# Half sums and differences of keys kept in two query buffers, and output halves added on VectorE

## The chip, the cores and the metric

The kernel runs on one core of one Trainium2 chip, in one launch. The core has five engines with instruction streams of their own: TensorE (PE, with its weight loads PEld), VectorE (DVE), ScalarE (ACT), GpSimd (POOL) and SyncE (SP), which only issues DMAs here. Each engine works through its stream in the order in which the program was written, and waits where a semaphore holds an instruction back. The metric is device time in microseconds, the median of several executions; the profile is one further execution.

## The reference

Two attention branches over the same 2048 x 512 input are mixed by a gate:

```
qkv = x @ wqkv                       # branch A: 32 heads of 16
logits = q . k[pos - 2*w], w = 0..7  # 8 keys behind each position, dilated by 2
a = softmax(logits) @ v @ wo_a
q = x @ wq; k = x @ wk; v = x @ wv   # branch B: 32 query heads, one key/value head
b = softmax(q k^T / 4) @ v @ wo_b    # all 2048 keys for all 2048 queries
out = g * a + (1 - g) * b            # g = sigmoid(x . gate_w)
```

Branch B is the bulk: 32 x 2048 x 2048 scores, their exponentials, and their sums weighted with v. All is float32.

## The kernel before

**Units and steps.** Branch B is cut into 32 units (NU): four blocks of 512 queries (NQB) times eight groups of four heads (NHG). A unit has 16 steps, one for each 128 keys, so phase 2 has 512 steps (NS). In each step `exp_pair` (line 443) makes scores for two pairs of heads, in the banks eb[0] and eb[1] (e0, e1), and ScalarE takes their exponentials into SBUF (tile pexp, six buffers); `weighted` (line 455) multiplies those of the step before with v and adds them up in the bank po. After a unit's 16 steps `finish_a` (line 470) transposes po on VectorE, and GpSimd scales it with the gate.

**Maxima.** Softmax subtracts the maximum over the keys, which must be known before a unit's first step. So all scores are computed twice: a *fill* is a matmul of 128 queries by 512 keys of one head (62 of the 64 rows of one half of the array; the two halves work side by side for the two heads of a couple) and a maximum over its 512 columns. There are 2048 fills (NF), 64 per unit. `fill_pair` (line 326) makes two in the double bank m2 with one reduce on VectorE (line 331); `fill_one` (line 335) makes one in the bank m1 (line 342). Results land in a small tile mx per unit, made by `unit_tile` (line 301). When a unit is full, `filled` (line 316) reduces it once more (lines 321, 323) and `shift_a` to `shift_d` write minus the maximum into two spare rows of the unit's query buffer, so that the scores come out shifted.

**Pairs.** During phase 1 (projections), fills may take another form: with half sums and half differences of two blocks of keys (tile kcd, made by `half_keys` and `half_parts`, lines 363 and 375), the maximum of two scores is the half sum plus the absolute half difference. `fill_diff` (line 392) makes two difference matmuls in m2 and two Abs on ScalarE into dd; `fill_sum` (line 404) makes one sum matmul in m1 or po and one fused add-and-maximum on VectorE. A pair covers four fills, and of each two columns of mx it writes only one. `paired` says when this form is possible: an even position, its half sums formed, nothing left over in `half`. Phase 1 ends by emptying `formed`.

**Query buffers.** Units sit in eight buffers qst (NB). `stack(u)` (line 277) loads unit u by four DMAs on SP's queue as soon as the unit eight before it has ended.

**The order of the work** is written out by a planner that runs while the program is built: it keeps a clock for PE, ACT and DVE (`clk`, `after`, with the durations in line 45) and emits a fill where a bank is free by that clock. In the loop from line 992 every step emits e0's scores, a fill in m2, e1's scores, a fill in m1 if the rest needs it (line 1023: `ahead` counts two fills for every step to come, and eleven for each output row to come), then the weighted sums. Each engine keeps exactly that order.

**Output blocks.** The 16 output rows of 128 tokens come in four blocks of four, between steps (`out_phase`, line 707). A block starts when the units that it needs are shaped, branch A's half is done, and the lead of the fills falls under LEAD units or a latest step is reached; `prepare` stands one step ahead of it. `stream` (line 670) runs the two halves of the array side by side over the row's items (24 for each half, 21 in the last block) and puts fills between them. `turn` transposes branch A's rows; `out_store` (line 650) copies both halves of the output bank to SBUF on ScalarE (line 654), adds them on GpSimd (line 658) and stores the row. The last block runs while the last units are still at work, and keeps its rows in SBUF (line 668) until the end.

**Branch A** runs on GpSimd throughout (`work`, line 832), which also loads the output weights (`extra`).

Of the kernel before, what the change touches and what calls it, by code (L numbers as in the profile page):

```python
# [6 lines left out]
F32 = mybir.dt.float32  # L7
# [6 lines left out]
P = 128  # L14
# [22 lines left out]
NB = 8  # L37
# [3 lines left out]
NH = NJ // 2  # L41
LEAD, M2S, M1S = 1.5, 0.5, 0.3

# [5 lines left out]
def gated_mix_kernel(ctx, tc, xt, wa, wk, wq, wo_a, wo_b, out):  # L49
# [15 lines left out]
    mk = cp.tile([P, 8], F32, name="mk")  # L65
    qst = [cp.tile([P, 2, 512], F32R, name=f"qst{k}") for k in range(NB)]

# [209 lines left out]
    def stack(u):  # L277
        qb, hg = divmod(u, NHG)
        for b in range(2):
            hi, lo = (qd[s, :, qb, 4 * hg + 2 * b:4 * hg + 2 * b + 2, :].rearrange("d c n -> d (c n)") for s in range(2))  # L280
            ap = [list(x) for x in hi.ap]
            twice = bass.AP(tensor=hi.tensor, offset=hi.offset, ap=[ap[0], [0, 2]] + ap[1:])
            dst = qst[u % NB].rearrange("p c n -> p (c n)").bitcast(F32)
# [17 lines left out]
    def unit_tile(v):  # L301
        if v not in mx:
            mx[v] = wp.tile([P, 2, 2, 4, 4], F32, name="mx", bufs=3)
            if v <= NB:
                nc.scalar.activation(mx[v].rearrange("p b i t k -> p (b i t k)"), ident[:, 0:64], AF.Identity, scale=0.0, bias=mk[:, 6:7])
            left[v] = NF // NU
        return mx[v]

    def max_mm(dst, v, pr, t, kc, odd):
        b = 64 * odd  # L310
        nc.tensor.matmul(dst, qst[v % NB][b:b + 62, pr, t * P:(t + 1) * P], kst[b:b + 62, kc * 512:(kc + 1) * 512], start=True, stop=True)  # L311

# [62 lines left out]
    def half_parts(g, keys):  # L375
        for x in range(2):
            nc.scalar.activation(kcd[0][:, g, x], hb[g][x], AF.Identity, scale=mk[:, 0:1])
            at = after("act", clk["pe"], 0.65)
        for x in range(2):
            parts = kcd[0][:, g, x]  # L380
            nc.vector.scalar_tensor_tensor(parts, hb[g][x], mk[:, 1:2], parts.bitcast(F32), op0=ALU.mult, op1=ALU.add)
            free[keys[x]] = after("dve", at + 0.1, 0.7) + 0.1
        formed.add(g)

    def paired():
        return len(slots) > 1 and slots[0][3] % 2 == 0 and slots[0][3] // 2 in formed and slots[1] == slots[0][:3] + (slots[0][3] + 1,) and fillable()

    def half_mm(dst, v, pr, t, kc, x, odd):
        b = 64 * odd
        nc.tensor.matmul(dst, qst[v % NB][b:b + 62, pr, t * P:(t + 1) * P], kcd[0][b:b + 62, kc // 2, x, :], start=True, stop=True)  # L390

    def fill_diff():
        v, pr, t, kc = slots.pop(0)
        slots.pop(0)
        for odd in range(2):
            half_mm(m2[:, odd, :], v, pr, t, kc, 1, odd)
        at = after("pe", 0, T_R) + T_LAT
        for odd in range(2):
            nc.scalar.activation(dd[0][:, odd], m2[:, odd, :], AF.Abs)  # L399
# [33 lines left out]
    def shift_d(v, ml, k):  # L433
        b, g = divmod(k, 4)
        dst = qst[v % NB][64 * b + 62:64 * b + 64].rearrange("x i (t q) -> x i t q", t=4).bitcast(F32)
# [7 lines left out]
    def exp_pair(s, pr):  # L443
        bank, key = eb[pr], f"e{pr}"
        u, kt = divmod(s, NJ)
        for odd in range(2):
            b = 64 * odd
            nc.tensor.matmul(bank[:, odd, :], kst[b:b + 64, kt * P:(kt + 1) * P], qst[u % NB][b:b + 64, pr, :], start=True, stop=True)  # L448
        e = px.tile([P, 2, 512], F32, name="pexp", bufs=6)
        nc.scalar.activation(e, bank, AF.Exp, scale=SCALE)  # L450
# [199 lines left out]
    def out_store(j, n, k):  # L650
        nonlocal pool
        del turned[j, 0], turned[j, 1]
        two = p2b[0].tile([P, 2, D], F32, name="two", bufs=2)
        nc.scalar.activation(two, eb[k], AF.Copy)
        free[f"e{k}"] = after("act", clk["pe"] + T_LAT, 0.92)
        pool = max(pool, 1e3 * clk["act"]) + 1300
        if n == C:
            nc.gpsimd.tensor_add(two[:, 0], two[:, 0], two[:, 1])
            nc.sync.dma_start(out[0].rearrange("(p j) d -> p j d", j=NJ)[:, j, :], two[:, 0])
        else:  # L660
            x = len(parts)
            if x < 2:
                spare.append(p2[0].tile([P, 512], F32, name="part", tag=("own", "tr8")[x], bufs=1))
            elif x == 2:
                own = p2[0].tile([P, 2, 512], F32, name="part", tag="pr", bufs=1)
                spare.extend([own[:, 0, :], own[:, 1, :]])
            parts[j] = spare[x]
            nc.gpsimd.tensor_add(parts[j], two[:, 0], two[:, 1])

# [36 lines left out]

    def out_phase(js, n):

# [13 lines left out]
        def done(at):  # L722
            x, j, i = at
            if i % 4 == 3:
                run_tasks()
                run_pool()
            if x == 0 and i == 1:
                turn(j, 1)
# [103 lines left out]
    def work():  # L832
# [38 lines left out]
        for i in range(0, len(order), 2):  # L871
# [17 lines left out]
            yield from load(i + 3)  # L889
            if p2b and extra:  # L890
                for f, a in extra.pop(0):
                    f(*a)
                yield 1300
        assert not extra
# [199 lines left out]
```

## Time and profile before

| | |
|---|---|
| median of 3 runs | 1521.74 us (1521.68 to 1521.97) |
| profiled execution | 1523.47 us |
| its span, first to last instruction | 1521.7 us |
| granted TensorE clock | 0.998 |
| phase 1 | to 282 us |
| output blocks | from 865, 1131, 1270 and 1426 us |
| last step | to 1508 us |

In the profile, `L331` is line 331 of the kernel, `mx<-pm` means that a tile mx is written from the bank pm, and `x562` counts instructions. The banks are named by their tiles: pe is e0 and e1, pm is m2, ps is m1. A row of a group has busy time and mean duration, then the idle time of the engine ahead of it with what ended it. In the timeline a row has start, duration, engine, line, operation; "[0.83 <-ACT mx L305]" says that the engine was idle for 0.83 us until that ACT instruction ended. A row of a window has its bounds and length, then busy time and number of instructions of each engine (or of one line's alone), the granted clock, the share of DMA time and GB/s.

### The profile page before, as it was taken

The numbers are of one execution on the slowest core, as the hardware profiler recorded it, in microseconds if no ns is written. First come the engines' busy times: TensorE is split into PE (matmuls) and PEld (weight loads), VectorE is DVE, ScalarE is ACT, GpSimd is POOL, SyncE is SP. The second block draws the span as 40 slices with busy tenths as digits, with TensorE's granted clock in tenths as the row PEclk, the third lists the DMA queues.
The fourth block names the chain that finished last, engine by engine and source line by source line (L and its number), as shares of the span: only waits on it lengthen the run. The fifth ranks groups of instructions, "written<-read, shape, count | busy, mean of one in ns | idle before, by whom it ended". The sixth has DMA issues, their size and how long they took to land.

```text
span 1521.7 us, 29098 instructions
## 1 busy us (share of the span) xinstructions
PE 1490.4 (98%) x11020; PEld 708.1 (47%) x11020; DVE 1236.0 (81%) x1748; ACT 1245.8 (82%) x1590; POOL 1035.8 (68%) x1773
## 2 busy tenths in 40 slices
PE   7999999999999999999999999999999999999998
PEld 4889888533333333333333453333345335433532
DVE  6976666789889888889888998898989889887811
ACT  4558987889999999999999759999974995799676
POOL 7866987787888888988888888889888003100210
PEclk9999999999999999999999999999999999999999
DMA  6744223121121120220211112102101000000000
GB/s 216 203 116 134 87 73 121 44 75 47 40 86 43 44 76 19 69 63 25 75 54 35 61 40 68 46 34 69 50 30 34 6 2 15 16 2 1 1 2 28
DMA packets 43908, 85.63 MB, mean 56 GB/s; under 512 B 9520, under 2 KB 25960, under 8 KB 39672
## 3 DMA queue, kind: packets, MB, share of 16 engines
q1 hardware_dynamic: 36200, 44.00, 9.7%
q0 software_dynamic: 6560, 37.95, 7.4%
q8 instruction: 86, 1.41, 0.4%
q10 hardware_dynamic: 1008, 1.84, 0.3%
q14 instruction: 54, 0.44, 0.1%
HBM read 57.97 MB, written 25.25 MB: 55 GB/s over the span
## 4 chain that ended last, share of the span: by engine, by line
PE 88%; ACT 6%; DVE 4%; issue 1%; DMA 1%; POOL 0%; SPq 0%; DVEq 0%; ACTq 0%; POOLq 0%
PE po L458 31%; PE pe L448 22%; PE pm L311 9%; PE pe L943 9%; PE ps L311 8%; PE pe L719 5%; ACT pexp L450 3%; ACT dd L399 2%; DVE mx L331 2%; PE pm L390 1%; PE pe L174 1%; PE po L390 1%; PE ps L390 1%; DVE mx L342 1%; DMA xraw<-xt 1%
## 5 line engine op out<-in xcount | busy, mean ns | idle before, releaser
L450 ACT ACTIVATE pexp<-pe 128x1024 f32<-128x1024 f32 x1024 | 991.8, 1022 | 93.1 <-PE pe L448 91.7
L331 DVE TENSOR_REDUCE mx<-pm 128x2 f32<-128x1024 f32 x562 | 686.3, 1221 | 134.3 <-PE pm L311 129.8
L458 PE MATMUL po<-pexp,vst 128*32 128x512 f32 x4096 | 545.5, 605 | 1.2 <-ACT pexp L450 0.6
L448 PE MATMUL pe<-qst,kst 64*128 64x512 f32 x2048 | 465.6, 450 | 7.1 <-ACT pexp L450 3.9
L448 PEld LDWEIGHTS pe<-qst,kst 64*128 64x128 f32 x2048 | 191.3, 183 | 513.5 <-ACT pexp L450 503.3
L342 DVE TENSOR_REDUCE mx<-ps 128x1 f32<-128x512 f32 x553 | 376.1, 680 | 4.9 <-PE ps L311 4.1
L311 PE MATMUL pm<-kst,qst 62*128 62x512 f32 x1137 | 237.8, 408 | 3.0 <-DVE mx L331 2.4
L311 PE MATMUL ps<-kst,qst 62*128 62x512 f32 x553 | 224.4, 406 | 0.8 <-DVE mx L342 0.8
L518 POOL TENSOR_TENSOR pr<-aext 128x256 f32<-128x256 f32 x256 | 182.0, 737 | 0.2
L578 POOL TENSOR_TENSOR oa<-oa,av 128x256 f32<-128x256 f32 x224 | 163.9, 732 | 15.4
L458 PEld LDWEIGHTS po<-pexp,vst 128*32 128x32 f32 x4096 | 80.6, 108 | 178.2 <-issue 164.9
L575 POOL TENSOR_TENSOR av<-aext,lg 128x256 f32<-128x256 f32 x224 | 139.2, 622 | 12.8
L484 POOL TENSOR_TENSOR rl<-rl,gate_t 128x16 f32<-128x16 f32 x31 | 6.8, 220 | 197.9 <-DVE rl L478 197.8
L311 PEld LDWEIGHTS pm<-kst,qst 62*128 62x128 f32 x1137 | 109.6, 186 | 26.8 <-DVE mx L331 22.6
L311 PEld LDWEIGHTS ps<-kst,qst 62*128 62x128 f32 x553 | 102.9, 186 | 25.4 <-DVE mx L342 20.3
L399 ACT ACTIVATE dd<-pm 128x512 f32<-128x512 f32 x166 | 92.2, 610 | 22.5 <-PE pm L390 11.4
L943 PE MATMUL pe<-wah,xh 64*128 64x384 f32 (+1 forms) x504 | 109.2, 343 | 0.0
L943 PE MATMUL pe<-wal,xh 64*128 64x384 f32 (+1 forms) x504 | 108.9, 341 | 0.0
L943 PE MATMUL pe<-wah,xl 64*128 64x384 f32 (+1 forms) x504 | 108.9, 341 | 0.0
L409 DVE CUSTOM_DVE_ANT_0 dd<-ps,dd 128x512 f32<-128x512 f32 x83 | 57.4, 692 | 60.5 <-PE ps L390 30.3
L250 POOL TENSOR_TENSOR stage<-stage,two 128x384 f32<-128x384 f32 x64 | 64.9, 1014 | 29.9 <-ACT two L241 15.5
L524 POOL TENSOR_TENSOR tr<-pr 128x512 f32<-128x512 f32 x64 | 81.7, 1276 | 4.2
(168 smaller groups left out, 1594.2 us busy)
## 6 DMA issues: line engine op xcount, KB each, us to landing
aext<-ad POOLq DMA_DIRECT2D x32, 1056.0 KB, 5.4
ad<-stage SPq DMA_DIRECT2D x32, 384.0 KB
qst<-qd SPq DMA_DIRECT2D x64, 128.0 KB
xraw<-xt SPq DMA_DIRECT2D x16, 256.0 KB
qd<-qhi SPq DMA_DIRECT2D x16, 256.0 KB
qd<-qlo SPq DMA_DIRECT2D x16, 256.0 KB
qst<-qd SPq DMA_DIRECT2D x64, 64.0 KB
qst<-ml SPq DMA_DIRECT2D x228, 2.0 KB
```

The lines of the kernel that those rows point to most:

```text
L311: nc.tensor.matmul(dst, qst[v % NB][b:b + 62, pr, t * P:(t + 1) * P], kst[b:b + 62, kc * 512:(kc + 1) * 512], start=True, stop=True)
L331: nc.vector.tensor_reduce(m[:, :, pr, t, kc], dst, AX.X, ALU.max)
L342: nc.vector.tensor_reduce(m[:, odd, pr, t, kc:kc + 1], dst, AX.X, ALU.max)
L399: nc.scalar.activation(dd[0][:, odd], m2[:, odd, :], AF.Abs)
L448: nc.tensor.matmul(bank[:, odd, :], kst[b:b + 64, kt * P:(kt + 1) * P], qst[u % NB][b:b + 64, pr, :], start=True, stop=True)
L450: nc.scalar.activation(e, bank, AF.Exp, scale=SCALE)
L458: nc.tensor.matmul(po[32 * i:32 * i + 32, :], vst[:, kt, :], pexp[s, i // 2][:, i % 2, :], start=(kt == 0), stop=(kt == NJ - 1))
L518: nc.gpsimd.tensor_mul(pr[:, k], q, e[:, o:o + NH, AC:2 * AC])
L524: nc.gpsimd.tensor_add(nx, cur[:, :, 0:n], cur[:, :, n:2 * n])
L575: nc.gpsimd.tensor_mul(av, e[:, o:o + NH, 2 * AC:].rearrange("p j (h d) -> p j h d", d=DH), lg[:, w].unsqueeze(3).to_broadcast([P, NH, AG, ...
L578: nc.gpsimd.tensor_add(ao, ao, av)
L943: nc.tensor.matmul(front[2 if x == last else x % 2][0][:, b, :n], l[h], r[h], start=(i == 0), stop=(i == 3 * C - 1))
```

## The change

Two stores keep the half sums and differences in DRAM while phase 1 makes them. At step 132 one load brings them back, over the two query buffers 6 and 7; from unit 14 on the units share the six others (`home`). Three output blocks, those of whole rows, start at the second step of a unit and take their fills as pairs, with the bank po (empty at that point) and with two dd tiles in turn. No single fill is made at the first step of a unit. Since pairs now occur among all units, every unit's mx gets its start value from ScalarE. `out_store` copies only one half of the bank, and VectorE adds the other to it. Blocks start at a lead of 3.0 instead of 1.5 units; the planner counts 20 fills for each whole row instead of eleven; GpSimd takes up to two loads of output weights at a time instead of one.

```diff
-LEAD, M2S, M1S = 1.5, 0.5, 0.3
+LEAD, M2S, M1S, PER_ROW = 3.0, 0.5, 0.3, 20
...
-    qst = [cp.tile([P, 2, 512], F32R, name=f"qst{k}") for k in range(NB)]
+    q67 = cp.tile([P, 2, 2, 512], F32R, name="q67")
+    qst = [cp.tile([P, 2, 512], F32R, name=f"qst{k}") for k in range(NB - 2)] + [q67[:, 0], q67[:, 1]]
+    kd = dp.tile([P, 2, 2, 512], F32, name="kd")
+
+    def home(v):
+
+        return (v % NB, v - NB) if v < 2 * NB - 2 else ((v - NB) % (NB - 2), v - NB + 2)
...
             mx[v] = wp.tile([P, 2, 2, 4, 4], F32, name="mx", bufs=3)
-            if v <= NB:
-                nc.scalar.activation(mx[v].rearrange("p b i t k -> p (b i t k)"), ident[:, 0:64], AF.Identity, scale=0.0, bias=mk[:, 6:7])
+            nc.scalar.activation(mx[v].rearrange("p b i t k -> p (b i t k)"), ident[:, 0:64], AF.Identity, scale=0.0, bias=mk[:, 6:7])
...
+        nc.sync.dma_start(kd[:, g], kcd[0][:, g].bitcast(F32))
         formed.add(g)
+
+    def half_back():
+
+        nc.sync.dma_start(q67.rearrange("p g x n -> p (g x n)").bitcast(F32), kd.rearrange("p g x n -> p (g x n)"))
+        kcd[0] = q67
...
+        dd.append(dd.pop(0))
         for odd in range(2):
             nc.scalar.activation(dd[0][:, odd], m2[:, odd, :], AF.Abs)
...
     def out_store(j, n, k):
-        nonlocal pool
         del turned[j, 0], turned[j, 1]
         two = p2b[0].tile([P, 2, D], F32, name="two", bufs=2)
-        nc.scalar.activation(two, eb[k], AF.Copy)
-        free[f"e{k}"] = after("act", clk["pe"] + T_LAT, 0.92)
-        pool = max(pool, 1e3 * clk["act"]) + 1300
-        if n == C:
-            nc.gpsimd.tensor_add(two[:, 0], two[:, 0], two[:, 1])
-            nc.sync.dma_start(out[0].rearrange("(p j) d -> p j d", j=NJ)[:, j, :], two[:, 0])
-        else:
+        nc.scalar.activation(two[:, 1], eb[k][:, 1], AF.Copy)
+        at = after("act", clk["pe"] + T_LAT, 0.5) + 0.1
+        free[f"e{k}"] = at + 1.5
+        if n < C:
...
-            nc.gpsimd.tensor_add(parts[j], two[:, 0], two[:, 1])
+        to = parts[j] if n < C else two[:, 0]
+
+        def rest():
+            nc.vector.tensor_add(to, eb[k][:, 0], two[:, 1])
+            free[f"e{k}"] = after("dve", at, 0.62) + 0.1
+            if n == C:
+                nc.sync.dma_start(out[0].rearrange("(p j) d -> p j d", j=NJ)[:, j, :], to)
+
+        tasks.append((at, rest, (), "sum"))
...
-    def out_phase(js, n):
+    def out_phase(js, n, whole_unit):
...
+            if x == len(js) - 1 and i == m - 5:
+                ended.add(1)
...
+        if whole_unit:
+            formed.update((0, 1))
+            free["po"] = max(free["po"], clk["dve"] + 0.1)
+            dd[:] = [px.tile([P, 2, 512], F32, name="pexp", bufs=6) for _ in range(2)]
         stream([(x, j, i) for x, j in enumerate(js) for i in range(m)], mm, done, False)
+        while pend:
+            odd = pend[0][4]
+            clk["pe"] = max(clk["pe"], free[("m1", "po")[odd]], ready_d[odd] - 0.3)
+            fill_sum()
+            clk["pe"] += T_R
+        settle("sum", 0)
+        formed.clear()
...
+        if s == 16 * NB + 4:
+            half_back()
-        if len(stacked) < NU and s > 16 * (len(stacked) - NB + 1):
+        if len(stacked) < NU and s > 16 * (home(len(stacked))[1] + 1):
             stack(len(stacked))
...
-        if due or outs < NJ and outs // NH in done and (NHG * (k + 1) - 1 in shaped if n == C else s >= 16 * (NU - 2) + 4) and (lead < LEAD or s >= 16 * (NHG * (k + 2) + 1) - 3):
+        if n == C:
+            ready = s and kt == 0 and outs // NH in done and NHG * (k + 1) - 1 in shaped and (lead < LEAD or s >= 16 * (NHG * (k + 2) + 1))
+        else:
+            ready = outs < NJ and s >= 16 * (NU - 2) + 4
+        if due or ready:
...
-                out_phase(list(range(outs, outs + 4)), due.pop())
+                out_phase(list(range(outs, outs + 4)), due.pop(), kt == 1)
...
-                ahead = 2 * (16 * (NU - 2) - 8 - s) + 11 * (NJ - 4 - outs)
-                if ahead < to_go() - NF // NU or s >= 16 * (NU - 2) - 8 and ahead + 64 < to_go():
+                ahead = 2 * (16 * (NU - 2) - 8 - s) + (PER_ROW if n == C else 11) * (NJ - 4 - outs)
+                if kt == 0 and s:
+                    pass
+                elif ahead < to_go() - NF // NU or s >= 16 * (NU - 2) - 8 and ahead + 64 < to_go():
                     fill_ready("m1", M1S)
```

Elsewhere `qst[v % NB]` becomes `qst[home(v)[0]]`.

More of the change, by code (lines that the diff above doesn't have):

```diff
@@ L282, in stack @@
             twice = bass.AP(tensor=hi.tensor, offset=hi.offset, ap=[ap[0], [0, 2]] + ap[1:])
-            dst = qst[u % NB].rearrange("p c n -> p (c n)").bitcast(F32)
+            dst = qst[home(u)[0]].rearrange("p c n -> p (c n)").bitcast(F32)
             nc.sync.dma_start(dst[64 * b:64 * b + 32], twice)
@@ L310, in max_mm @@
         b = 64 * odd
-        nc.tensor.matmul(dst, qst[v % NB][b:b + 62, pr, t * P:(t + 1) * P], kst[b:b + 62, kc * 512:(kc + 1) * 512], start=True, stop=True)
+        nc.tensor.matmul(dst, qst[home(v)[0]][b:b + 62, pr, t * P:(t + 1) * P], kst[b:b + 62, kc * 512:(kc + 1) * 512], start=True, stop=True)
     def to_go():
@@ L389, in half_mm @@
         b = 64 * odd
-        nc.tensor.matmul(dst, qst[v % NB][b:b + 62, pr, t * P:(t + 1) * P], kcd[0][b:b + 62, kc // 2, x, :], start=True, stop=True)
+        nc.tensor.matmul(dst, qst[home(v)[0]][b:b + 62, pr, t * P:(t + 1) * P], kcd[0][b:b + 62, kc // 2, x, :], start=True, stop=True)
     def fill_diff():
@@ L434, in shift_d @@
         b, g = divmod(k, 4)
-        dst = qst[v % NB][64 * b + 62:64 * b + 64].rearrange("x i (t q) -> x i t q", t=4).bitcast(F32)
+        dst = qst[home(v)[0]][64 * b + 62:64 * b + 64].rearrange("x i (t q) -> x i t q", t=4).bitcast(F32)
         (nc.gpsimd if b and not pieces else nc.sync).dma_start(dst[:, :, :, 32 * g:32 * g + 32], ml[32 * g + 16 * b:32 * g + 16 * b + 16, :].bitcast(F32))
@@ L447, in exp_pair @@
             b = 64 * odd
-            nc.tensor.matmul(bank[:, odd, :], kst[b:b + 64, kt * P:(kt + 1) * P], qst[u % NB][b:b + 64, pr, :], start=True, stop=True)
+            nc.tensor.matmul(bank[:, odd, :], kst[b:b + 64, kt * P:(kt + 1) * P], qst[home(u)[0]][b:b + 64, pr, :], start=True, stop=True)
         e = px.tile([P, 2, 512], F32, name="pexp", bufs=6)
@@ L889, in work @@
             yield from load(i + 3)
[L890 to L893, printed above, removed]
+            for _ in range(2):
+                if p2b and extra:
+                    for f, a in extra.pop(0):
+                        f(*a)
+                    yield 1300
         assert not extra
```

## The prediction

> **What bounds the kernel now.** I read the page first, then the timeline of single steps, then the groups cut into windows, and last the waits.
>
> ```profile
> span 1521.7 us, 29098 instructions
> ...
> PE 1490.4 (98%) x11020; PEld 708.1 (47%) x11020; DVE 1236.0 (81%) x1748; ACT 1245.8 (82%) x1590; POOL 1035.8 (68%) x1773
> ...
> L450 ACT ACTIVATE pexp<-pe 128x1024 f32<-128x1024 f32 x1024 | 991.8, 1022 | 93.1 <-PE pe L448 91.7
> L331 DVE TENSOR_REDUCE mx<-pm 128x2 f32<-128x1024 f32 x562 | 686.3, 1221 | 134.3 <-PE pm L311 129.8
> ```
>
> A busy share of 98% hides two kinds of step. In the timeline, the start of the weighted sums (L458) marks a step; columns are start and duration in us:
>
> ```profile
> 704.68 1.06 PE L458 MATMUL po<-pexp,vst 128*32 128x512 f32 x8
> 706.81 1.06 PE L458 MATMUL po<-pexp,vst 128*32 128x512 f32 x8
> ```
>
> ```profile
> 1400.28 3.83 ACT L450 ACTIVATE pexp<-pe 128x1024 f32<-128x1024 f32 x4 [0.19 <-PE pe L448]
> 1400.58 1.07 PE L458 MATMUL po<-pexp,vst 128*32 128x512 f32 x8
> 1402.70 1.07 PE L458 MATMUL po<-pexp,vst 128*32 128x512 f32 x8
> 1404.60 1.06 PE L458 MATMUL po<-pexp,vst 128*32 128x512 f32 x8
> ```
>
> A step with a pair of fills in m2 and a single fill in m1 takes 706.81 - 704.68 = 2.13 us and TensorE bounds it. Without the single, two steps take 1404.60 - 1400.58 = 4.02 us, 2.01 each, though TensorE alone could do one in 1.90 (1404.60 - 1402.70): four exponentials take 3.83 us plus a wait of 0.19, so ScalarE bounds it. One single fill taken out of such a step is therefore worth **0.12 us**, not its full 0.23. Nearly all steps have one: in the windows of the exponentials (first two rows; two per step) and of the single fills (last two):
>
> ```profile
> 283.00:863.00 580.00, 518.55 (x536) 1.00 0.17 54
> 1375.00:1423.00 48.00, 45.30 (x48) 1.00 0.01 2
> ...
> 283.00:863.00 580.00, 185.39 (x274) 1.00 0.17 54
> 1375.00:1423.00 48.00, 3.26 (x5) 1.00 0.01 2
> ```
>
> 580 us hold 268 steps with 274 singles (2.16 a step), 48 us hold 24 steps with 5 (2.00).
>
> The other stage is the output blocks. The three full ones, all engines (PE, PEld, DVE, ACT, POOL), then the fill matmuls of the first, then two of its waits (total, times, longest), then a run of output matmuls in the chain of waits:
>
> ```profile
> 865.10:898.60 33.50, 33.34 (x283) 22.80 (x279) 32.06 (x39) 11.02 (x18) 31.28 (x48) 1.00 0.07 25
> 1130.80:1164.40 33.60, 32.41 (x282) 23.31 (x280) 32.04 (x38) 10.42 (x16) 30.61 (x43) 1.00 0.07 25
> 1270.30:1303.30 33.00, 32.87 (x282) 22.83 (x280) 32.30 (x36) 9.91 (x15) 12.89 (x11) 1.00 0.07 25
> ...
> 865.10:898.60 33.50, 15.42 (x53) 6.49 (x53) 1.00 0.07 25
> ...
> PEld pm L311 <- DVE mx L331: 3.5, 11, 0.5
> PEld ps L311 <- DVE mx L342: 2.2, 8, 0.3
> ...
> 1449.75 4.23 PE pe L719 x36
> ```
>
> A block has 4 x 24 x 2 = 192 output matmuls; two of half height run together, 4.23 / 18 = 0.235 us a couple. With 53 fills that is 245 / 2 x 0.235 = 28.8 us of some 33.4; the other 4.6 are transposes, the two ends, and waits on VectorE, which is busy for 32 of 33.5 us. ScalarE idles for two thirds of it.
>
> **The change, part by part.** *Fills moved into the blocks.* In the blocks four maxima become one pair: two difference matmuls, two Abs on ScalarE, two sum matmuls, two fused reduces. This stood in phase 1 (166 Abs are 83 pairs in 173 us, 2.08 us a pair beside the projections):
>
> ```profile
> 107.00:280.00 173.00, 92.06 (x166) 0.99 0.33 101
> ...
> 200.57 1.09 ACT L399 ACTIVATE dd<-pm 128x512 f32<-128x512 f32 x2 [0.60 <-PE pm L390]
> ...
> 199.51 0.69 DVE L409 CUSTOM_DVE_ANT_0 dd<-ps,dd 128x512 f32<-128x512 f32 x1 [0.74 <-ACT dd L399]
> ...
> 200.13 0.69 DVE L409 CUSTOM_DVE_ANT_0 dd<-po,dd 128x512 f32<-128x512 f32 x1
> ...
> PEld pm L390 <- ACT dd L399: 14.1, 38, 2.3
> ```
>
> TensorE's work per fill is unchanged (four matmuls for four); VectorE's falls from two reduces of 1.22 to two of 0.62 apart; ScalarE gets 1.09. By the planner's constants a pair spans seven slots of 0.23 us, 1.61 us, in which five output items go, so 24 items carry at most 4.8 pairs, 19 fills a row; ScalarE's copies in a row (own, raw, turned, half of the output) cost some of that. I take 18 a row, 72 a block, bounds 60 and 80. Above the 54 of now that is 18 more: 18 / 2 x 0.235 = 2.1 us per block, **+6.3** for three (bounds +2 and +9). VectorE's load then is 18 x 1.24 + 4 x 0.69 = 25 us, ScalarE's 18 x 1.09 and 16 copies of a half bank at some 0.55 (half of the 1.09) 28, in 35.5, so neither is the bound; waits on Abs (14.1 us in 173, a twelfth) take the place of those on VectorE (5.7 in 33.5, a sixth), and I leave the 4.6 us as they are; from 2 us less to 5 us more a block is open.
>
> The 54 singles saved in steps give 54 x 0.12 = **-6.5** (bounds -2 and -9). So a fill costs in a block (0.117) what it frees in a step (0.12): this trade is worth nothing as long as ScalarE stands at 2.01.
>
> *No single at the first step of a unit*, about 26 steps while singles run: there the lone 1.90 step has ScalarE's slack around it and gains up to 0.23, and its fill is made up later at 0.12: 26 x 0.08 = **-2** (bounds 0 and -3).
>
> *Output halves.* ScalarE copies 512 columns instead of 1024, GpSimd's addition goes, VectorE does it:
>
> ```profile
> L658 POOL TENSOR_TENSOR two<-two 128x512 f32<-128x512 f32 x12 | 15.4, 1287 | 20.1 <-ACT two L654 20.1
> ...
> L1063 DVE TENSOR_TENSOR osl<-pe,part 128x512 f32<-128x512 f32 x4 | 2.6, 686 | 0.8 <-PE pe L1059 0.7
> ```
>
> 1.29 us on GpSimd becomes 0.69 on VectorE, 16 times, within the blocks, hidden under TensorE in the three paired ones. In the last, unpaired block VectorE is near full, and the last bank of each block is held by copy plus addition instead of one copy: **+0.5** in all (bounds -1 and +4).
>
> *The start value of the maxima.* Now only units 0 to 8 get it from ScalarE; afterwards all 32, since a pair writes one of two columns. That is 23 more of these, and two of the nine fell among steps (columns: least, median and greatest ns, first and last start):
>
> ```profile
> L305 ACT ACTIVATE mx<-ident,mk x9: 333/348/389, 26.6 to 338.0; 128x64 f32<-128x64 f32 x9
> ```
>
> ```profile
> 336.44 0.50 PE L448 MATMUL pe<-qst,kst 64*128 64x512 f32 x2
> ...
> 337.95 0.34 ACT L305 ACTIVATE mx<-ident,mk 128x64 f32<-128x64 f32 x1
> ...
> 338.33 1.23 DVE L331 TENSOR_REDUCE mx<-pm 128x2 f32<-128x1024 f32 x1 [0.83 <-ACT mx L305]
> 338.57 0.51 PE L448 MATMUL pe<-qst,kst 64*128 64x512 f32 x2
> 339.61 0.18 PEld L311 LDWEIGHTS pm<-kst,qst 62*128 62x128 f32 x2 [0.85 <-DVE mx L331]
> 341.62 0.49 PE L448 MATMUL pe<-qst,kst 64*128 64x512 f32 x2
> ```
>
> ```profile
> 290.73 0.50 PE L448 MATMUL pe<-qst,kst 64*128 64x512 f32 x2
> 293.58 0.51 PE L448 MATMUL pe<-qst,kst 64*128 64x512 f32 x2
> ...
> 616.91 0.50 PE L448 MATMUL pe<-qst,kst 64*128 64x512 f32 x2
> 617.40 0.29 DVE L321 TENSOR_REDUCE ms<-mx 128x32 f32<-128x128 f32 x1
> 619.03 0.50 PE L448 MATMUL pe<-qst,kst 64*128 64x512 f32 x2
> ```
>
> The start value is issued with a unit's first fill, so it queues on ScalarE behind the exponential of that step; the first reduce waits for it (0.83 us), the next pair of fills waits in TensorE's program order for that reduce, and behind it stand the next scores. The steps took 341.62 - 338.57 = 3.05 and 293.58 - 290.73 = 2.85 us, 0.92 and 0.72 over 2.13; a change of unit without it took 619.03 - 616.91 = 2.12. Since TensorE bounds these steps, nothing gives it back. I take 0.82 for 17 units that start among steps with singles, 0.7 for 4 that start in blocks, 0.4 for 2 later ones: **+17.5** (bounds 23 x 0.3 = 7 and 23 x 1.0 = 23).
>
> The Trainium skill, "ScalarE: Activation LUTs", What happens when an exp ACTIVATE runs, gives an ACTIVATE with a pointer bias 280 ns + 0.833 ns per element, 333 ns for these 64; the trace's 348 agrees. Priced by that alone the 23 would be 8 us, an estimate from that page; the steps quoted show that the place in the queue costs more than the instruction.
>
> *The rest, at nothing.* Two stores of the half keys in phase 1 and one load of 1 MB at step 132 go on SP's queue; unit 7 ended at step 127, and the first reader is the first block, at 865 us now, some 300 us after step 132: that is the cover; were it gone, one block would wait a few us. Six query buffers instead of eight allow fills a shorter lead; should that limit bite, a few steps go without fills that later ones take up, at the 0.12 us for which they were freed. Earlier blocks and doubled weight loads move work under TensorE.
>
> Sum: 6.3 - 6.5 - 2 + 0.5 + 17.5 = **+15.8 us** on a span of 1521.7. The profiled execution took 1523.47 with 1.8 us around the span; the median is 1521.74, so the forecast is 1521.74 + 15.8 = 1537.5.
>
> **The rivals.** *(1) Faster: relief of VectorE decides.* If each block loses 3.4 of its 4.6 us because VectorE falls from 32 to 25 us (its waits were 5.7, partly covered), full blocks take 32.1 instead of 35.5 us, 1.2 less than now: sum -6.5 - 2 + 0.5 - 3 x 1.2 = -11.6 plus 23 times the price of a start value. It wins if that price is below 0.37, for instance the instruction's own 0.35, hidden behind nothing: -3.6, 1518; at zero, 1510. For it: VectorE's waits of 5.7 us a block. Against: 0.92 and 0.72.
>
> *(2) The start value costs only its 0.348 us*, the blocks as forecast: -1.7 + 8.0 = +6.3, 1528. For it: units that start in blocks or late steps; against: the same two steps.
>
> *(3) The chain of the pairs bounds the blocks:* at phase 1's 2.08 us, 18 pairs take 37.4 us, with 3 at the ends 40.4, 7 more than now: 6.3 becomes 21, 1552. For it: Abs, reduce and bank follow one another, and ScalarE also makes the copies. Against: two dd buffers instead of one.
>
> *(4) Few pairs form* (odd positions, a half left over): with 54 fills a block neither the 6.3 nor the 6.5 arises, 1537.7: only counts, not the time, would tell.
>
> **How the numbers follow.** Forecast 0.45 and (4) 0.05, both near 1537; (3) 0.16; (2) 0.13; (1) 0.21, of which 0.06 lies within 0.2%. About 0.2%, 3 us, is what a measurement of this kernel can tell from no change. So faster 0.15, same 0.06, slower 0.79. The likeliest case's own range is 1529 to 1546; the range with (2), (3) and the upper part of (1) is 1518 to 1553.
>
> **What would show it.** Right: 32 start values, most with a step of 2.8 to 3.1 us behind them; about 36 sum matmuls in each of three blocks of 35 to 36 us; VectorE near 25 us there; single fills ending some 50 steps earlier; steps still at 2.13 and 2.01. Wrong: unit starts at 2.2 us, blocks of 33 or of 40 us, or steps below 1.95 without singles.

## The result and the profile after

The changed kernel takes 1522.6 us in the median (1520.7 to 1526.4, 20 runs) against 1521.7 us (1520.3 to 1523.9, 20 runs): a ratio of 1.0008 [1.0001, 1.0014], +0.9 us. The prediction was slower by 15.8 us; its range holds the time, its forecast and its main chance are wrong. The change makes no difference of 0.2%.

The page of the changed kernel, lines that answer to those of before:

```profile
span 1520.0 us, 29435 instructions
...
PE 1481.2 (97%) x11020; PEld 708.3 (47%) x11020; DVE 1196.1 (79%) x1806; ACT 1291.3 (85%) x1713; POOL 1014.0 (67%) x1753
...
L336 DVE TENSOR_REDUCE mx<-pm 128x2 f32<-128x1024 f32 x520 | 634.6, 1220 | 153.3 <-PE pm L316 142.6
```

TensorE lost 9 us of busy time, VectorE 40, and ScalarE gained 45: the trade that the change makes. The total hardly moved, so where it was given back has to be read from stages. The three output blocks of whole rows, each with the step that it stands in, by windows (PE, PEld, DVE, ACT, POOL, granted clock, DMA share, GB/s):

```profile
763.20:800.60 37.40, 35.81 (x309) 27.19 (x307) 30.07 (x84) 29.75 (x60) 33.19 (x56) 1.00 0.16 57
935.90:972.70 36.80, 35.49 (x307) 25.52 (x305) 30.00 (x82) 28.69 (x56) 32.77 (x54) 1.00 0.08 29
1210.90:1249.10 38.20, 36.61 (x312) 26.17 (x310) 30.40 (x80) 29.10 (x56) 16.69 (x22) 1.00 0.10 33
```

Less their step of 2.1 us they take 34.7 to 36.1 us, as forecast (35 to 36); VectorE is busy for 30 us, not 25. In the waits of the first block two rows stand that have no counterpart in the prediction: the scores after the block wait for VectorE's addition of output halves (total, times, longest). Behind all four blocks these waits are 6.0 and 4.3 us; before, the same scores waited 4.4 and 2.9 us for ScalarE's copy.

```profile
PEld pe L460 <- DVE two L679: 1.5, 1, 1.5
...
PE pe L460 <- DVE two L679: 1.1, 1, 1.1
```

The waits of VectorE between 282 and 1400 us show the start values (L310 is the line of the start value, L336 and L347 the reduces, L421 the fused one):

```profile
DVE mx L336 <- ACT mx L310: 5.4, 6, 1.4
DVE mx L347 <- ACT mx L310: 5.4, 14, 0.8
DVE pexp L421 <- ACT mx L310: 2.3, 2, 1.6
```

That is 13.1 us; before, the same view had two waits of 0.8. Two changes of unit in the timeline, first one as the prediction had it, then another:

```profile
528.11 1.06 PE L470 MATMUL po<-pexp,vst 128*32 128x512 f32 x8
528.49 0.34 ACT L310 ACTIVATE mx<-ident,mk 128x64 f32<-128x64 f32 x1
...
528.86 1.23 DVE L336 TENSOR_REDUCE mx<-pm 128x2 f32<-128x1024 f32 x1 [0.86 <-ACT mx L310]
...
530.14 0.19 PEld L316 LDWEIGHTS pm<-kst,qst 62*128 62x128 f32 x2 [0.85 <-DVE mx L336]
...
531.16 1.07 PE L470 MATMUL po<-pexp,vst 128*32 128x512 f32 x8
```

```profile
429.84 1.07 PE L470 MATMUL po<-pexp,vst 128*32 128x512 f32 x8
...
431.12 0.35 ACT L310 ACTIVATE mx<-ident,mk 128x64 f32<-128x64 f32 x1
...
431.50 0.69 DVE L347 TENSOR_REDUCE mx<-ps 128x1 f32<-128x512 f32 x1 [0.23 <-ACT mx L310]
...
434.38 0.64 PE L470 MATMUL po<-pexp,vst 128*32 128x512 f32 x4
```

The first step took 531.16 - 528.11 = 3.05 us, 0.92 over 2.13. In the second place, two steps took 434.38 - 429.84 = 4.54 us, 0.28 over 2 x 2.13: the planner had left out a single fill there, VectorE had time, and its reduce waited for 0.23 us only. Nine of the 18 starts among steps are of the second kind; their two steps together are from 0.05 us shorter to 0.47 longer than 2 x 2.13, 0.21 in the mean.

The table sums the distances between successive starts of the weighted sums in the profiled executions: the four blocks, each with its step, all other steps, and the single fills in these (counted by their reduces). Its last column runs from the first weighted sum to the end of the profile. The four blocks grew by 4.2 us (6.8 forecast with the output halves), the steps lost 2.6 (9.0 more were forecast). Ratios are to the kernel before in the same runs.

| kernel | median us | ratio | blocks | steps | singles in steps | from phase 2 on |
|---|---|---|---|---|---|---|
| before | 1521.7 | 1 | 139.4 | 1087.7 | 457 | 1239.2 |
| after | 1522.6 | 1.0008 [1.0001, 1.0014] | 143.6 | 1085.1 | 402 | 1240.5 |
| e1_early | 1510.3 | 0.9925 [0.9912, 0.9937] | 142.9 | 1076.5 | 402 | 1231.3 |
| e2_init_alone | 1535.1 | 1.0091 [1.0075, 1.0106] | 139.3 | 1101.0 | 457 | 1252.6 |
| e3_skip_alone | 1524.0 | 1.0013 [1.0004, 1.0022] | 139.4 | 1089.7 | 435 | 1241.4 |
| e4_no_pairs | 1544.1 | 1.0146 [1.0132, 1.0159] | 134.6 | 1115.7 | 434 | 1262.3 |
| e5_no_skip | 1528.4 | 1.0049 [1.0036, 1.0061] | 143.6 | 1091.3 | 405 | 1246.7 |
| e6_old_store | 1516.7 | 0.9967 [0.9955, 0.9980] | 137.7 | 1085.0 | 420 | 1234.6 |
| e7_early_skip2 | 1513.7 | 0.9949 [0.9936, 0.9961] | 143.6 | 1078.8 | 401 | 1234.6 |
| e8_init_alone_early | 1521.4 | 0.9996 [0.9987, 1.0005] | 139.3 | 1089.2 | 457 | 1240.7 |
| e9_early_old_store | 1505.8 | 0.9894 [0.9881, 0.9908] | 137.3 | 1077.8 | 420 | 1226.9 |
| e10_early_copy_both | 1508.4 | 0.9913 [0.9899, 0.9926] | 138.8 | 1078.2 | 420 | 1229.1 |
| e11_early_store_no_skip | 1510.9 | 0.9928 [0.9914, 0.9941] | 137.2 | 1082.3 | 424 | 1231.4 |

The profiled span of before is 1.7 us longer than that of after, though after's blocks and steps together take 1.6 us more: before's phase 1 took 282.4 us, against 279.5. One stretch of before's phase 1, and the same of after:

```profile
80.00:110.00 30.00, 28.22 (x260) 26.01 (x259) 20.25 (x33) 15.71 (x46) 16.82 (x31) 0.94 0.39 103
```

```profile
80.00:110.00 30.00, 28.28 (x275) 26.03 (x273) 21.35 (x37) 16.36 (x48) 18.34 (x33) 1.00 0.48 140
```

The granted clock was 0.94 there in that execution. Of the other kernels, e2_init_alone has the phase 1 of before unchanged and takes 279.5 us. So this difference isn't the change's, and profiles are compared from phase 2 on.

### The profile page after: what moved, and what is told of

Its sections match the earlier page's. It is cut to its first block, busy times and chain, and to the rows that moved or that the text cites. A ratio compares the mean times of both kernels' runs of the same rounds, so it can differ in the third digit from the quotient of the medians.

```text
span 1520.0 us, 29435 instructions
## 1 busy us (share of the span) xinstructions
PE 1481.2 (97%) x11020; PEld 708.3 (47%) x11020; DVE 1196.1 (79%) x1806; ACT 1291.3 (85%) x1713; POOL 1014.0 (67%) x1753
## 4 chain that ended last, share of the span: by engine, by line
PE 82%; ACT 9%; DVE 4%; POOL 3%; issue 2%; DMA 0%; SPq 0%; DVEq 0%; ACTq 0%; POOLq 0%
PE po L470 29%; PE pe L460 20%; PE pe L973 9%; PE pm L316 7%; PE ps L316 6%; ACT pexp L462 5%; PE pe L735 4%; PE pm L401 2%; ACT dd L411 2%; DVE mx L336 2%; PE pe L180 1%; PE ps L401 1%; PE po L401 1%; DVE mx L347 1%; POOL oa L590 1%
## 5 line engine op out<-in xcount | busy, mean ns | idle before, releaser
L336 DVE TENSOR_REDUCE mx<-pm 128x2 f32<-128x1024 f32 x520 | 634.6, 1220 | 153.3 <-PE pm L316 142.6
L470 PE MATMUL po<-pexp,vst 128*32 128x512 f32 x4096 | 545.5, 605 | 0.3 <-ACT pexp L462 0.3
L460 PE MATMUL pe<-qst,kst 64*128 64x512 f32 x1920 | 437.8, 453 | 10.4 <-ACT pexp L462 6.1
L460 PEld LDWEIGHTS pe<-qst,kst 64*128 64x128 f32 x1920 | 179.3, 183 | 491.5 <-ACT pexp L462 472.9
L347 DVE TENSOR_REDUCE mx<-ps 128x1 f32<-128x512 f32 x445 | 302.3, 679 | 9.5 <-ACT mx L310 5.4
L316 PE MATMUL pm<-kst,qst 62*128 62x512 f32 x997 | 203.6, 400 | 7.0 <-DVE mx L336 6.8
L316 PE MATMUL ps<-kst,qst 62*128 62x512 f32 x421 | 167.6, 398 | 2.1 <-DVE mx L347 2.1
L470 PEld LDWEIGHTS po<-pexp,vst 128*32 128x32 f32 x4096 | 80.6, 108 | 173.1 <-issue 162.8
L587 POOL TENSOR_TENSOR av<-aext,lg 128x256 f32<-128x256 f32 x224 | 139.3, 622 | 13.1
L316 PEld LDWEIGHTS pm<-kst,qst 62*128 62x128 f32 x997 | 96.0, 186 | 18.4 <-DVE mx L336 16.4
L421 DVE CUSTOM_DVE_ANT_0 dd<-ps,dd 128x512 f32<-128x512 f32 x83 | 57.4, 692 | 58.9 <-PE ps L401 27.6
L316 PEld LDWEIGHTS ps<-kst,qst 62*128 62x128 f32 x421 | 78.5, 187 | 13.3 <-DVE mx L347 7.7
```

The costliest lines, as they stand in the source:

```text
L316: nc.tensor.matmul(dst, qst[home(v)[0]][b:b + 62, pr, t * P:(t + 1) * P], kst[b:b + 62, kc * 512:(kc + 1) * 512], start=True, stop=True)
L336: nc.vector.tensor_reduce(m[:, :, pr, t, kc], dst, AX.X, ALU.max)
L347: nc.vector.tensor_reduce(m[:, odd, pr, t, kc:kc + 1], dst, AX.X, ALU.max)
L470: nc.tensor.matmul(po[32 * i:32 * i + 32, :], vst[:, kt, :], pexp[s, i // 2][:, i % 2, :], start=(kt == 0), stop=(kt == NJ - 1))
L587: nc.gpsimd.tensor_mul(av, e[:, o:o + NH, 2 * AC:].rearrange("p j (h d) -> p j h d", d=DH), lg[:, w].unsqueeze(3).to_broadcast([P, NH, AG, ...
```

## The experiments

**Start values one unit early** (on the changed kernel). The instruction stays, its place moves: it is issued when the unit before gets its first fill.

```diff
     def unit_tile(v):
-        if v not in mx:
-            mx[v] = wp.tile([P, 2, 2, 4, 4], F32, name="mx", bufs=3)
...
+        for u in (v, v + 1):
+            if u < NU and u not in left:
+                mx[u] = wp.tile([P, 2, 2, 4, 4], F32, name="mx", bufs=3)
...
```

> The changed kernel, with each unit's start value of the maxima issued on ScalarE one unit earlier, at the first fill of the unit before, so that the same 32 instructions remain and no first reduce waits for one. Theory (the place in ScalarE's queue is the price): changes of unit take 2.1 to 2.4 us instead of 2.8 to 3.1, some 7 us less among the steps and 1 to 2 in the blocks, so 7 to 9 us less than the changed kernel, near 1514. Rival (the start value costs its own 0.35 us of ScalarE wherever it stands): within 1.5 us of the changed kernel, near 1522.

Measured 1510.3 us, 12.3 less than after, where I had expected 7 to 9. The same change of unit as above, in the timeline of this kernel:

```profile
524.50 1.06 PE L471 MATMUL po<-pexp,vst 128*32 128x512 f32 x8
524.63 0.34 ACT L311 ACTIVATE mx<-ident,mk 128x64 f32<-128x64 f32 x1
...
526.27 1.23 DVE L337 TENSOR_REDUCE mx<-pm 128x2 f32<-128x1024 f32 x1 [0.43 <-PE pm L317]
...
526.63 1.07 PE L471 MATMUL po<-pexp,vst 128*32 128x512 f32 x8
```

The start value lies among the exponentials as before, for 0.34 us, but no reduce waits for it, and the step takes 2.13 us instead of 3.05 (the step ahead of it, not shown, takes 2.38). Blocks and steps together lose 9.3 us. Another 1.9 us go in phase 1, which ends at 277.6 instead of 279.5 us: there the fused reduces waited five times for a start value, 5.4 us in all, and with the early place they don't. These seven start values of phase 1 stood in the kernel before too, so this part was no cost of the change.

**All 32 start values in the kernel before**, at a unit's first fill (the diff), and one unit early (with the edit above):

```diff
             mx[v] = wp.tile([P, 2, 2, 4, 4], F32, name="mx", bufs=3)
-            if v <= NB:
-                nc.scalar.activation(mx[v].rearrange("p b i t k -> p (b i t k)"), ident[:, 0:64], AF.Identity, scale=0.0, bias=mk[:, 6:7])
+            nc.scalar.activation(mx[v].rearrange("p b i t k -> p (b i t k)"), ident[:, 0:64], AF.Identity, scale=0.0, bias=mk[:, 6:7])
```

> The kernel before with one part of the change alone: all 32 units get a start value from ScalarE at their first fill. Theory of the prediction: 23 more at 0.82 us, 1537 to 1541. Revised theory from the changed kernel's steps (0.2 to 0.9 us, by whether a unit begins with a pair in m2 or with a single in m1 and whether the planner drops a single behind it): 8 to 14 us, 1530 to 1536. Rival (own time on ScalarE only, which has slack in these steps): 1522 to 1525.

> The kernel before with all 32 start values, each issued a unit early. Theory (the wait is the price, not ScalarE's 0.35 us): within 2 us of the kernel before, 1520 to 1524, against 1535 when issued at the first fill. Rival (ScalarE's own time counts): 1527 to 1530.

Measured 1535.1 and 1521.4 us: +13.3 and nothing. So 23 more start values cost 13.3 / 23 = **0.58 us** each at the first fill; the last column of the table gives 13.3 too. The price is the wait of VectorE's reduce, of the fills behind it, and of the scores behind these. The nothing is a net of two things, since the nine start values that the kernel already had moved as well: phase 1 ends 1.8 us earlier than in e2_init_alone (277.7 against 279.5), and the two changes of unit among the steps, 2.85 and 3.05 us before, became 2.13 and 2.36; against that, from phase 2 on the kernel takes 1.5 us more than before. So the 23 cost some (1.5 + 1.4) / 23 = 0.13 us each a unit earlier, an estimate from these profiles, and not 0.58.

**No single at the first step, in the kernel before:**

```diff
-                if ahead < to_go() - NF // NU or s >= 16 * (NU - 2) - 8 and ahead + 64 < to_go():
+                if kt == 0 and s:
+                    pass
+                elif ahead < to_go() - NF // NU or s >= 16 * (NU - 2) - 8 and ahead + 64 < to_go():
```

> The kernel before with one part of the change alone: no single fill in the first step of a unit. Theory: each of some 29 such steps saves 0.23 to 0.27 us, and its single is made up late for 0.12, so 3 to 4.5 us less, 1517.5 to 1519. Rival of the prediction (0.08 each): 1519.5 to 1520. Rival (VectorE's transposes set these steps anyway): no change, 1521 to 1523.

Measured 1524.0 us, slower by 2.2: a miss. First steps, with the two behind each, became some 6.5 us shorter in all, but singles then ran to the last step that may hold them and didn't suffice, so that the planner stopped the steps for fills alone, at 1390.5 us. The window of this pause (columns as above):

```profile
1390.50:1400.20 9.70, 5.42 (x26) 1.99 (x25) 8.41 (x8) 2.75 (x4) 0.00 (x0) 0.79 0.00 1
```

In 9.7 us VectorE was the bound (8.41 busy, 8 instructions), TensorE was busy for 56%, and its granted clock fell to 0.79.

**The changed kernel with singles at first steps again:**

```diff
-                if kt == 0 and s:
-                    pass
-                elif ahead < to_go() - NF // NU or s >= 16 * (NU - 2) - 8 and ahead + 64 < to_go():
+                if ahead < to_go() - NF // NU or s >= 16 * (NU - 2) - 8 and ahead + 64 < to_go():
```

> The changed kernel with single fills allowed again in the first step of a unit. Theory (a step without a single saves 0.23 to 0.27 us where it stands alone, and 0.12 in the run of such steps at the end): some 27 first steps grow by 0.25, and the singles end some 27 steps earlier at 0.12: 3 to 4 us slower than the changed kernel, about 1526. Rival of the prediction (0.08 net each): 2 us slower. Rival (VectorE's transposes set these steps): no change.

Measured 1528.4 us, 5.8 more than after, where I had expected 3 to 4. The rows of a first step in the timeline, after (L470 weighted sums, L484 the transposes of po), and then with the single:

```profile
450.54 1.07 PE L470 MATMUL po<-pexp,vst 128*32 128x512 f32 x8
452.43 1.06 PE L470 MATMUL po<-pexp,vst 128*32 128x512 f32 x8
453.57 0.72 DVE L484 STREAM_TRANSPOSE tt<-po 128x512 f32<-128x512 f32 x1
454.79 1.07 PE L470 MATMUL po<-pexp,vst 128*32 128x512 f32 x8
456.92 0.64 PE L470 MATMUL po<-pexp,vst 128*32 128x512 f32 x4
```

```profile
452.31 1.07 PE L470 MATMUL po<-pexp,vst 128*32 128x512 f32 x8
454.44 1.07 PE L470 MATMUL po<-pexp,vst 128*32 128x512 f32 x8
455.21 0.68 DVE L347 TENSOR_REDUCE mx<-ps 128x1 f32<-128x512 f32 x1
455.81 0.71 DVE L484 STREAM_TRANSPOSE tt<-po 128x512 f32<-128x512 f32 x1
456.57 1.07 PE L470 MATMUL po<-pexp,vst 128*32 128x512 f32 x8
458.95 0.64 PE L470 MATMUL po<-pexp,vst 128*32 128x512 f32 x4
```

With the single, its reduce at 455.21 stands ahead of the transposes, the reduces behind them are late, and the second step takes 458.95 - 456.57 = 2.38 us. Without it the three steps take 456.92 - 450.54 = 6.38 us, with it 458.95 - 452.31 = 6.64: a quarter of a us.

**Is it the lone step or the transposes?** The early start value, and no single at the first and the ninth step of a unit:

```diff
-                if kt == 0 and s:
+                if kt % 8 == 0 and s:
                     pass
```

> The run with early start values, with no single in the first and the ninth step of a unit. Theory: another 27 steps stand alone without a single and save 0.23 each, the singles end some 29 steps later, near step 466, still ahead of the deadline, at 0.12 each: 2.5 to 3.5 us less than with early start values, about 1507.3. Rival (the fills no longer fit and a pause comes, as in the run with the first steps left out of the kernel before): 4 us or more slower.

Measured 1513.7 us, 3.3 more than e1_early: a miss. A ninth step in the timeline, TensorE and ScalarE:

```profile
1048.21 1.06 PE L471 MATMUL po<-pexp,vst 128*32 128x512 f32 x8
1050.11 1.07 PE L471 MATMUL po<-pexp,vst 128*32 128x512 f32 x8
1052.47 1.06 PE L471 MATMUL po<-pexp,vst 128*32 128x512 f32 x8
...
1049.81 3.84 ACT L463 ACTIVATE pexp<-pe 128x1024 f32<-128x1024 f32 x4 [0.20 <-PE pe L461]
```

1.90 and 2.36 us are 2 x 2.13: four exponentials in a row take 3.84 us, and the next step pays back what the lone one gained. Singles displaced here cost their 0.12 later. At first steps the gain is the collision with the transposes that goes.

**The changed kernel without pairs:**

```diff
-LEAD, M2S, M1S, PER_ROW = 3.0, 0.5, 0.3, 20
+LEAD, M2S, M1S, PER_ROW = 3.0, 0.5, 0.3, 12
...
-                out_phase(list(range(outs, outs + 4)), due.pop(), kt == 1)
+                out_phase(list(range(outs, outs + 4)), due.pop(), False)
```

> The changed kernel without pairs in the output blocks: they take single and paired-bank fills as before, and the planner counts 12 fills a row instead of 20. Theory (a fill costs in a block what it frees in a step): blocks 2 us shorter each, steps longer by 54 singles at 0.12, together within 2 us of the changed kernel. Rival (the pairs are what pays): 4 us or more slower than the changed kernel. Rival (the pairs' chain costs): 3 us or more faster.

Measured 1544.1 us, 21.5 more than after, where I had expected nothing. The three blocks became shorter (34.1 to 34.7 us with their step), with 46 to 48 fills each, but the other fills no longer fitted into the steps. Windows of the two pauses:

```profile
1359.10:1372.20 13.10, 7.78 (x32) 2.75 (x31) 11.78 (x11) 3.03 (x4) 0.00 (x0) 0.77 0.01 3
1406.50:1421.50 15.00, 9.16 (x36) 3.68 (x35) 13.54 (x13) 2.46 (x4) 0.00 (x0) 0.63 0.00 1
```

28 us of pauses, less the two steps in them, outweigh 9.0 us of shorter blocks, and the other steps take 6.6 us more, 32 singles x 0.12 = 3.8 of it. So the pairs pay for the room that they make, which the first steps without singles use up.

**The old output halves** in the changed kernel (`out_store` of before), alone and with the early start values:

```diff
-        nc.scalar.activation(two[:, 1], eb[k][:, 1], AF.Copy)
+        nc.scalar.activation(two, eb[k], AF.Copy)
...
-            nc.vector.tensor_add(to, eb[k][:, 0], two[:, 1])
+            nc.gpsimd.tensor_add(parts[j], two[:, 0], two[:, 1])
```

> The changed kernel with the output halves copied both by ScalarE and added by GpSimd, as before the change. Theory: the addition is hidden on either engine, and only the ends of the blocks differ: within 1.5 us of the changed kernel. Rival (ScalarE is near its limit in the paired blocks, so 0.4 us more a row counts): 2 to 6 us slower. Rival (the addition on VectorE costs): 2 us or more faster.

> The changed kernel with two edits together: start values of the maxima issued one unit early, and the output halves as before (ScalarE copies both halves, GpSimd adds). Theory: the two costs lie in different places (unit starts among the steps; output blocks), so the gains add: 1510.3 - 5.9 = 1504.4 us, blocks 137 to 138 us in all, unit starts as with the early start value alone. Rival: they overlap, since a unit's start value falls into a block or since singles displaced by one come back in the other; then between 1506 and 1510.

Measured 1516.7 us, 5.9 less than after, where I had expected 1.5 at most either way, and 1505.8 us, 4.5 less than e1_early: the two costs nearly add, and e9_early_old_store is the fastest of all, 16.0 us under before. What part of the new halves costs? With the early start values, both halves copied by ScalarE and VectorE adding from SBUF:

```diff
-        nc.scalar.activation(two[:, 1], eb[k][:, 1], AF.Copy)
+        nc.scalar.activation(two, eb[k], AF.Copy)
...
-            nc.vector.tensor_add(to, eb[k][:, 0], two[:, 1])
+            nc.vector.tensor_add(to, two[:, 0], two[:, 1])
```

> Start values one unit early; ScalarE copies both halves of the output bank as before the change (1024 columns, bank free after the copy), but the addition stays on VectorE, from SBUF. It splits the cost of the output-half edit, 5.9 us in the blocks. Theory B (the bank, held through copy and addition in turn, and the scores that wait for it at a block's end): the cost goes, 1504 to 1506 us, and no wait of the next scores for the addition is left. Theory V (VectorE's time and place in its program, 16 x 0.69 us among its reduces): the cost stays, 1509 to 1511 us.

Measured 1508.4 us, between the two. Who waited in the changed kernel for the additions (L679), and in e9_early_old_store for the copies (L667), total and times:

```profile
  PEld pe L460: 6.0, 4
  PE pe L460: 4.3, 4
```

```profile
  PEld pe L461: 4.8, 4
...
  PE pe L461: 3.0, 4
```

The scores after the four blocks wait 1.2 to 1.3 us longer in all for the bank, about a quarter of the cost. The additions themselves cost something too (1508.4 against 1505.8), and longer blocks also carry more fills (402 singles in steps against 420, 18 x 0.12 = 2.2 us that come back). By the medians 1.9 us go to the bank and 2.6 to VectorE, by the last column of the table 2.2 each; the intervals of the medians are too near to each other to settle the division.

**The moved fills alone:** the edits of e1_early, e6_old_store and e5_no_skip together. What stays of the change goes with the fills: pairs, half keys in two query buffers, earlier blocks, more loads of output weights at a time.

> Start values one unit early, output halves as before the change, and single fills allowed at the first step of a unit again: what is left of the change is the moved fills alone (pairs in three blocks, their keys in two query buffers, blocks one or more units earlier). Theory of the prediction (a fill costs in a block what it frees in a step): 1521.7 - 0.2 = 1521.5 us. Theory C, that the pairs free the blocks of their waits on VectorE so that the 54 added fills are carried there at no more time than before: 54 x 0.12 = 6.5 us and the shorter blocks 2.0 us, 1511 to 1513 us.

Measured 1510.9 us, 10.8 less than before. Its first block by windows, and then the first two waits of TensorE's weight loads there:

```profile
797.10:832.20 35.10, 34.24 (x300) 26.31 (x299) 24.99 (x68) 28.02 (x50) 33.99 (x47) 1.00 0.18 60
```

```profile
PEld pe L732 <- ACT turned L641: 1.4, 3, 0.5
PEld pe L461 <- ACT two L667: 1.1, 1, 1.1
```

The waits for VectorE's reduces, 3.5 and 2.2 us in the prediction's rows of before, aren't among them, and VectorE is busy for 25.0 us instead of 32. The blocks hold 63 to 66 fills (before 54 to 57) and are 2.2 us shorter in all; the steps lose 5.3 us, 33 singles x 0.12 = 4.0 of it and some 1.4 the two changes of unit that the early start values shorten. With 0.4 of the tail after the last step that makes 7.9 by the profile. The rest of the median lies in phase 1, as far as is known: 282.4 against 279.2 us in the profiled executions, by the early start values and by the granted clock. e8_init_alone_early, which has the same start values and nothing else of the change, is the closer comparison: 1521.4 - 1510.9 = 10.5 us by the medians and 1240.7 - 1231.4 = 9.3 from phase 2 on.

## Why the prediction was wrong, by its steps

The runs give a ladder, each rung a difference of two medians, so that the rungs must add up; beside it stands the same difference of the table's last column:

| step of the prediction | forecast | medians | from phase 2 on | from |
|---|---|---|---|---|
| fills moved (+6.3 and -6.5) | -0.2 | -10.8 | -7.9 | e11 against before |
| no single at the first step | -2 | -5.1 | -4.4 | e9 against e11 (5.8 by e5) |
| output halves | +0.5 | +4.5 | +4.4 | e1 against e9 (5.9 by e6) |
| start values | +17.5 | +12.3 | +9.2 | after against e1 (13.3 by e2) |
| sum | +15.8 | +0.9 | +1.3 | |

The first and the fourth rung differ between the columns since the early start values also shorten phase 1, by some 2 us.

**The step that failed** is "this trade is worth nothing as long as ScalarE stands at 2.01", and within it "I leave the 4.6 us as they are". A step's side of it was right: 0.12 us a fill. In the block I charged 0.117 us for each added fill as if TensorE had no idle time there, though I had quoted 5.7 us of waits on VectorE. These went with the pairs, and little took their place: the added fills run in what had been waits. Their price in a block was below zero, not 0.117: in e11_early_store_no_skip the blocks give -2.2 us where +6.3 was forecast, and the singles saved give -4.0 where -6.5 was. That is the mechanism of rival (1), at about half of its size: it let each block lose 3.4 us of its own, with 18 fills added; with 9 or 10 added the blocks are 0.8 us shorter each, so they lost 0.8 + 9.3 x 0.117 = 1.9. I had that rival's VectorE row and its condition; what I didn't do is to let the block's own idle time pay for the fills in the forecast.

**Start values.** The mechanism was right: same wait, same 0.92 us in steps such as the one quoted. The term was mis-sized: I took 0.82 for all 17 from two steps, both at a place with a single behind. In the changed kernel the planner drops a single behind half of the starts, and there the two steps take only 0.21 us more in the mean. In e2_init_alone most starts do show steps of 2.6 to 3.3 us, but at some of these places a step had taken 2.5 to 2.7 without a start value, so that less was added. Measured 12.3 to 13.3 instead of 17.5; the lower bound of 7 and the upper of 23 held. Rival (2), 0.348 each, falls: 13.3 / 23 = 0.58, and some 0.13 where no reduce waits. The duration of an ACTIVATE that the prediction quotes from the Trainium skill, "ScalarE: Activation LUTs", stands there in the section What ACT_TABLE_LOAD costs.

**No single at the first step.** Right in sign, for the wrong reason. "The lone 1.90 step has ScalarE's slack around it" isn't so (e7_early_skip2: 1.90 + 2.36); the gain is VectorE's, whose transposes no longer collide with a reduce. It needs the pairs' room: without them it cost 2.2 us (e3_skip_alone).

**Output halves.** "Hidden under TensorE in the three paired ones" failed: 4.5 to 5.9 us instead of 0.5, over the upper bound of +4. I had named the bank held by copy plus addition at each block's end, but within 0.5 us for everything; the scores behind the four blocks wait 1.2 to 1.3 us longer for it than with the old halves. How the rest divides between the bank and VectorE's time stays open.

**Right** were 32 start values, 68 to 73 fills a block (72 forecast), steps at 2.13 and 2.01, and the rest, of which no run shows a cost. VectorE in a block was at 25 us only with the old halves. Singles ended at step 438 instead of 463, 25 earlier and not 50. Rivals (3) and (4) fell: blocks less their step take 35 to 36 us, and 16 or 17 pairs form in each. That the time still lies in the range is in part luck: three of the four terms were off the same way, by 18.9 us in all, and one the other way by 4.0, and the range reached down to 1518 only for the sake of rivals (1) and (2). Rival (1) with 0.58 us for a start value would give -11.6 + 13.3 = +1.7, near the result as well, but its other terms, -6.5 for the singles, -2 and +0.5, were measured at -4.0, -5.1 and +4.5.

## What to carry to other kernels

A block in which the bound engine waits has room: price work added there first against those waits, and only the rest in busy time. A small instruction on an in-order queue costs what waits for it; before removing it, try to issue it earlier, which here was worth 12 us for an edit of a few lines, some 2 of them in phase 1, where the old kernel had the same waits. Where a change has several parts of both signs, each part needs a run of its own: 16 us of gain and 17 of loss looked like nothing.

## What the runs showed of the hardware

Gaps of under a microsecond were enough to lower TensorE's granted clock. In the pauses of e4_no_pairs TensorE was idle for 0.6 us between two pairs of fills,

```profile
1362.03 0.49 PE L316 MATMUL pe<-kst,qst 62*128 62x512 f32 x2 [0.66 <-DVE mx L336]
```

and windows of TensorE alone in the first pause, ahead of the fall of the clock and behind it, give:

```profile
1361.00:1366.00 5.00, 2.38 (x10) 1.00 0.00 2
1367.00:1376.00 9.00, 6.86 (x27) 0.50 0.01 2
```

Five us with gaps of 0.63 to 0.66 us, busy for 48%, went ahead of the fall; the one longer gap of this pause, 1.47 us, came behind it, at 1369.6. Over the whole pauses the clock was 0.77 and 0.63. The Trainium skill, "TensorE: Matmul & The Clock Gate", warns of idle gaps of more than some 3.4 us (section HAM oscillation) and, as a second kind, of frequent small gaps between groups of matmuls (section A second HAM failure mode: psum-queue depth-cycling). These runs agree with the second, at gaps of 0.6 us.

VectorE's addition of 512 columns took 0.68 to 0.69 us with one operand in PSUM (L679 in the changed kernel), but with both in SBUF it took longer in some blocks. The windows of the three blocks of whole rows in e10_early_copy_both, first the additions alone (time and number), then all engines (GpSimd last, ahead of the clock):

```profile
755.70:792.20 36.50, 4.03 (x4) 1.00 0.15 53
926.50:962.80 36.30, 5.15 (x4) 1.00 0.09 30
1199.70:1234.50 34.80, 2.76 (x4) 1.00 0.09 31
```

```profile
755.70:792.20 36.50, 35.09 (x305) 26.46 (x303) 29.46 (x80) 29.72 (x55) 33.16 (x53) 1.00 0.15 53
926.50:962.80 36.30, 35.19 (x303) 25.38 (x301) 29.82 (x75) 28.32 (x52) 33.31 (x52) 1.00 0.09 30
1199.70:1234.50 34.80, 34.08 (x304) 25.61 (x306) 25.88 (x68) 27.17 (x48) 13.94 (x16) 1.00 0.09 31
```

1.01 and 1.29 us each with GpSimd busy for 33 of 36 us, 0.69 with 14 of 35. The Trainium skill, "SBUF — State Buffer", SBUF: two separate sides, says that VectorE with two SBUF inputs and a GpSimd instruction that reads SBUF share a pair of ports, which one of them holds for a whole instruction. These numbers fit: the addition is lengthened in the two blocks in which GpSimd is busy throughout, though not by the same time in both. It may be part of what VectorE's addition cost in that run; no run separates it.
